# Large loads of a cached-attention decode kernel carried half by SyncE's queue and half by ScalarE's

## The chip, the cores and the metric

The kernel runs on one core of a Trainium2 chip. The metric is the device time of one execution in microseconds (us), taken as the median over runs. The engines are named as in the profile: PE is TensorE, DVE is VectorE, ACT is ScalarE, POOL is GpSimd, SP is SyncE. A transfer (DMA) is issued by an engine's instruction stream, here by SP's or ACT's, and is carried by 16 DMA engines that all transfers of the core share. Each issuing engine has one queue on each DMA engine. "Entries" below are what such a queue holds: one packet for each contiguous row of a transfer that falls to that DMA engine, and one more that counts the transfer's semaphore up.

## The reference, cut to what matters

One decode step (one query token for each of two sequences) of grouped attention over a long cache, times a gated small network:

```python
# x: (2, 1, 512); k_cache, v_cache: (2, 8, 32768, 128) bf16, 134 MB each
xn = layernorm(x)
q  = xn @ wq                                   # 32 heads of 128; 4 heads share one of the 8 cache heads
scores = einsum("bhqd,bhkd->bhqk", q, k) * 128 ** -0.5
o  = einsum("bhqk,bhkd->bhqd", softmax(scores), v)
s  = o.reshape(2, 1, 4096) @ wo                # wo: 4096 x 512
# B, with one token: the shifted quarters of its first stage are all zero, so x1 = xn
b  = xn + gelu(layernorm(xn) @ w3) @ w4        # w3: 512 x 1792, w4: 1792 x 512
out = x + s * silu(b)
```

Nearly all bytes are K and V, each read once: 280.5 MB in all with the weights.

## The kernel before, in words

There are 16 groups, one for each pair of sequence and cache head. A group's K is 32768 x 128 bf16, which is 8 MB: 128 partitions of 64 KB each, cut into two parts of 32 KB (`NPART = 2`, a part is a `SLOT`). Its V has the same shape. `kbuf` has three slots, so the next group's K can be loaded as soon as the first part of the present one is used up; `vbuf` has two, so the next V waits until the present V is used up.

For each group DVE transposes K in 16 pieces (line 493), PE multiplies them with the query (line 562, scores in `sc`), DVE finds the maximum (lines 476 to 503), ACT takes the exponential (line 417), DVE transposes the result (line 511), PE multiplies with V (line 584, sum in `o`), and ACT copies `o` out to `ob` (line 420). PE's part of a group is one loop body that is run 16 times. After the last group PE multiplies the collected outputs with `wo` (lines 608 and 615), DVE makes the last two products (lines 520 and 521), and SP and ACT each store one row.

All large loads are issued by SP, in the order of the code, each behind the event that frees its buffer:

- at the start `wq`, `w3`, `w4` and K of group 0, with no wait (lines 252 to 255). `wq` lies in the third slot of `kbuf`; `w3` and `w4` lie in `vbuf`.
- V of group 0 behind `e_h2`, the last matmul that reads `w4` (line 387).
- K of group m behind `s_half` reaching m: PE gives it when it has used the first part of K of group m - 1 (line 398).
- V of group m behind `s_pv` reaching m: PE gives it when it has used V of group m - 1 (line 387).
- K and V of the last group as two parts each (lines 404 and 392), and then `wo` in seven parts (line 411), which lies where K was.

ACT issues small transfers only: `x` (line 258), four pieces of `x` spread over partitions into `x4_bf` (line 270, "x4" below; two rows of 256 bytes each), four pieces of the gate `g` into `g4` (line 379; two rows of 512 bytes each), and half of the output. The engines' instruction streams run in order. DVE's stream has, between the prologue and its loop over the groups, a copy of `x4_bf` that waits for the four x4 transfers (line 380), and behind it two memsets (lines 381 and 382), of which PE's loop waits for the second:

```python
e_x4 = ve.op(lambda v: v.tensor_copy(out=x4[:, :], in_=x4_bf[:, :]), (d_x4, 16 * NQ))
ve.op(lambda v: v.memset(qrb[:, :], 0.0), e_qr)
e_s0 = ve.op(lambda v: v.memset(pro[:, :], 0.0))
```

DVE's loop then begins a group by waiting for K's semaphore `t_k[i]`. A transfer adds 16 to its semaphore, one for each DMA engine, and `take(..., 16)` waits for that and subtracts it.

Of the kernel before, what the change touches and what calls it, by code (L numbers as in the profile page):

```python
# [94 lines left out]
def kernel(  # L95
# [14 lines left out]
    nc = tc.nc  # L110

    B, Sq, D = A_x.shape
    _, Hkv, Sk, Dh = A_k_cache.shape
    HD = A_wq.shape[1]
# [94 lines left out]

    groups = [(b, k) for b in range(B) for k in range(Hkv)]  # L210
    NG = len(groups)
    wo_parts = [(0, 4, 0, NQ), (4, 5, 0, NQ), (5, 6, 0, NQ), (6, 7, 0, NQ), (7, 8, 0, 2), (7, 8, 2, 3), (7, 8, 3, NQ)]
    KC = 2
    PAD = 24

    def sem(name):
        return tc.alloc_semaphore(name)
# [1 line left out]
    def row_view(cache, b, k):  # L219
        return cache[b, k, :, :].rearrange("(p t) d -> p (t d)", p=128)  # L220
# [26 lines left out]
    def order(m):  # L247
        return (1, 0) if m % 2 == 0 else (0, 1)

    with tc.tile_critical(sync_engine=mybir.EngineType.Pool, no_gpsimd_drain=True):  # L250

        sp.op(lambda e: e.dma_start(out=kbuf_wq[:, 0:DK * HD], in_=A_wq.rearrange("(p k) f -> p (k f)", k=DK)), inc=(d_wq, 16))
        sp.op(lambda e: e.dma_start(out=vbuf[:, 0:W4O], in_=B_w3.rearrange("(p k) f -> p (k f)", k=DK)), inc=(d_w3, 16))
        sp.op(lambda e: e.dma_start(out=vbuf[:, W4O:W4O + FK * D], in_=B_w4.rearrange("(p f) d -> p (f d)", f=FK)), inc=(d_w4, 16))
        sp.op(lambda e: e.dma_start(out=kbuf[:, 0:NPART * SLOT], in_=row_view(A_k_cache, *groups[0])), inc=(t_k[0], 16))
        nc.sync.sem_inc(t_k[1], 16)

        ac.op(lambda e: e.dma_start(out=x_bf[:, :], in_=A_x[:, 0, :]), inc=(d_x, 16))
        e_x4z = po.op(lambda e: e.memset(x4_bf[:, :], 0.0))
        e_xs0 = po.op(lambda e: e.memset(xs_bf[:, :], 0.0))  # L260
        e_id0 = po.op(lambda e: e.memset(ident[:, :], 0.0))
# [70 lines left out]
        for i in range(NPART):  # L332
            for k in range(DK):
                for n in range(NQ):
                    last = k == DK - 1 and n == NQ - 1
                    e = pe.op(lambda t, i=i, k=k, n=n: t.matmul(  # L336
                        sc[i][32 * n:32 * n + B, :], lhsT=xT[:, k, :],
                        rhs=wq3[:, k, :].rearrange("p (h n y) -> p h n y", n=NQ, y=32)[:, i * HH:(i + 1) * HH, n, :],
                        start=(k == 0), stop=(k == DK - 1), tile_position=(0, 32 * n)),
                        e_xT, e_s00, (d_wq, 16), inc=last)  # L340
            e = ve.op(lambda v, i=i: v.transpose(out=qT[:, i * 512:(i + 1) * 512], in_=sc[i][:, :]), e)
        e_q = ve.op(lambda v: v.tensor_mul(
            out=q_sb[:, :, :, :].rearrange("p n e (b h) -> p (n e) b h", b=B),
# [10 lines left out]
        for k in range(DK):  # L354
            for n in range(NQ):
                last = k == DK - 1 and n == NQ - 1
                e = pe.op(lambda t, k=k, n=n: t.matmul(
                    pro[32 * n:32 * n + B, 0:FQ], lhsT=xT[:, DK + k, :],
                    rhs=w3v[:, k, n * FQ:(n + 1) * FQ].rearrange("p (y f) -> p f y", y=32),
                    start=(k == 0), stop=(k == DK - 1), tile_position=(0, 32 * n)), (d_w3, 16), inc=last)  # L360
        e = ve.op(lambda v: v.transpose(out=h4[:, :], in_=pro[:, 0:FQ]), e)
        e_hf = ve.op(lambda v: v.tensor_copy(
            out=hf[:, :].rearrange("p (f b) -> p f b", b=B), in_=h4[:, :].rearrange("p (f c) -> p f c", c=32)[:, :, 0:B]), e)
# [7 lines left out]
        for f in range(FK):  # L371
            e_h2 = pe.op(lambda t, f=f: t.matmul(  # L372
                h2[0:B, :], lhsT=h_bf[:, f * B:(f + 1) * B], rhs=w4v[:, f, :],
                start=(f == 0), stop=(f == FK - 1)), e, (d_w4, 16), inc=f == FK - 1)
        e_tf = ve.op(lambda v: v.tensor_add(out=t_f[:, :], in0=xn[:, :], in1=h2[0:B, :]), e_h2)
        e = ac.op(lambda v: v.activation(out=sig[:, :], in_=t_f[:, :], func=ACT.Sigmoid), e_tf)
        e_g = ve.op(lambda v: v.tensor_mul(out=g[:, :], in0=t_f[:, :], in1=sig[:, :]), e)
        for n in range(NQ):
# [3 lines left out]
        e_s0 = ve.op(lambda v: v.memset(pro[:, :], 0.0))  # L382


        def load_v(m, *events):
            if m < NG - 1:
                sp.op(lambda e: e.dma_start(out=vbuf[:, :], in_=row_view(A_v_cache, *groups[m])), *events, inc=(t_v[0], 16))
                nc.sync.sem_inc(t_v[1], 16)
                return
            for h in range(NPART):  # L390
                c = slice(h * SLOT, (h + 1) * SLOT)
                sp.op(lambda e, c=c: e.dma_start(out=vbuf[:, c], in_=row_view(A_v_cache, *groups[m])[:, c]), *events, inc=(t_v[h], 16))  # L392

        load_v(0, e_h2)
        for m in range(1, NG):
            base = m % 2
            if m < NG - 1:
                sp.op(lambda e, m=m, base=base: e.dma_start(
                    out=kbuf[:, base * SLOT:(base + NPART) * SLOT], in_=row_view(A_k_cache, *groups[m])),
                    (s_half, m), e_q, inc=(t_k[0], 16))  # L400
                nc.sync.sem_inc(t_k[1], 16)
            else:
                for i, h in enumerate(order(m)):
                    sp.op(lambda e, m=m, h=h, base=base: e.dma_start(
                        out=kbuf[:, (base + h) * SLOT:(base + h + 1) * SLOT],
                        in_=row_view(A_k_cache, *groups[m])[:, h * SLOT:(h + 1) * SLOT]),
                        (s_half, m), inc=(t_k[i], 16))
            load_v(m, (s_pv, m))
        for i, (a, c, r0, r1) in enumerate(wo_parts):
            cols = slice(r0 * D, r1 * D)  # L410
            sp.op(lambda e, a=a, c=c, cols=cols: e.dma_start(out=wo3[:, a:c, cols], in_=wos[:, a:c, cols]), (s_pv, NG - 1), inc=(d_wo[i], 16))  # L411


        for m in range(NG):
            for h in range(NPART):
                i = order(m).index(h)
                ac.op(lambda v, i=i: v.activation(  # L417
                    out=ep[i][:, :], in_=sc[i][:, :], func=ACT.Exp, scale=inv_sqrt_dh, bias=shift[:, :], accum_out=rs[:, i:i + 1]),
                    (s_shift, m + 1), e_tf if m == 0 else None, inc=(t_e, 1))
            ac.op(lambda v: v.copy(out=ob[:, :], in_=o[:, :]), (s_pv, m + 1), inc=(t_ob, 1))  # L420

        z_cols = z[:, :, :, (NR - 1) * rep:].rearrange("p n e c -> p (n e) c")
        z_cols = z_cols[:, :, 0:128].rearrange("p w (j c) -> p w j c", j=4)[:, :, :, 0:rep]
# [58 lines left out]
        with nc.Fori(0, NG // 2, engines=[DVE], hint_back_edge=True):  # L482
            for par in range(2):
                take(nc.vector, t_z)
                for i, h in enumerate(order(par)):
                    take(nc.vector, t_k[i], 16)
                    u = par + h
                    kt = kbuf[:, u * SLOT:(u + 1) * SLOT].bitcast(I32)
                    for r in range(NR):
                        n = i * NR + r  # L490
                        if n >= T_BUFS:
                            take(nc.vector, t_used)
                        nc.vector.transpose(  # L493
                            out=Ts[n % T_BUFS][:, :].rearrange("p (b t k) -> p t b k", b=NB, t=RT),
                            in_=kt[:, r * W:(r + 1) * W].rearrange("p (t b k) -> p t b k", b=NB, t=RT)).then_inc(t_T, 1)
                        if i == 1 and r == 3:
                            peak(0)
                            head_on()
                head_out()
                take(nc.vector, t_used, T_BUFS)  # L500
                peak(1)
                take(nc.vector, t_top)
                nc.vector.tensor_reduce(  # L503
                    out=shift[:, :], in_=S[:, NPART * rep:], axis=AX.X, op=ALU.min).then_inc(s_shift, 1)
                for h in range(NPART):
                    take(nc.vector, t_e)
                    if h == NPART - 1:
                        nc.vector.tensor_mul(
                            out=sm[:, :, :], in0=sel_h[:, :].unsqueeze(1).broadcast_to([128, NPART, rep]),
                            in1=rs[:, :].unsqueeze(2).broadcast_to([128, NPART, rep]))  # L510
                    nc.vector.transpose(  # L511
                        out=pt[h][:, :, :].rearrange("p r (t h) -> p t r h", h=rep),
                        in_=ep[order(par).index(h)][:, :].rearrange("p (t r h) -> p t r h", r=NR, h=rep)).then_inc(t_pt, 1)
# [36 lines left out]
        with nc.body("pe_groups", valid_engines=[PE]):  # L550
# [24 lines left out]
                S[:, NPART * rep:], lhsT=same_h[:, :], rhs=mxr[:, :, :].rearrange("p i r -> p (i r)"),  # L575
                start=True, stop=True).then_inc(t_top, 1)
            for h in range(NPART):
                take(nc.tensor, t_v[h], 16)
                take(nc.tensor, t_pt)
                vt = vbuf[:, h * SLOT:(h + 1) * SLOT].rearrange("p (t d) -> p t d", d=Dh)  # L580
                for u in range(KPT // VT):
# [16 lines left out]
        with nc.body("pe_output", valid_engines=[PE]):  # L598
# [3 lines left out]
            for i, (a, c, r0, r1) in enumerate(wo_parts):  # L602
                for k in range(a, c):
                    pe.wait(e_oX[(B - 1) * Hkv + k], (d_wo[i], 16))
                    for r in range(r0, r1):
# [7 lines left out]
                        for n in range(NQ):  # L613
# [2 lines left out]
                                pro[32 * n:32 * n + B, 0:QW], lhsT=oX[:, k, r, :], rhs=wo3[:, k, col:col + QW],  # L616
                                start=(gr == KC * NQ), stop=(gr == Hkv * NQ - 1), tile_position=(0, 32 * n)),
                                inc=(gr == Hkv * NQ - 1 and n == NQ - 1))
                if i == 0:
                    take(nc.tensor, t_on)  # L620
                    head_xp()
                    for n in range(NQ):
# [41 lines left out]
```

## Time and profile before

| What | Value |
|---|---|
| median of 3 runs | 658.0 us (657.98 to 658.12) |
| the profiled execution | 657.31 us |
| its span, first to last instruction | 655.5 us |
| HBM read | 280.50 MB, 428 GB/s over the span |
| PE busy / DVE busy / ACT busy | 62% / 58% / 6% of the span |
| packets of SP's queue (q1) | 6728, 280.50 MB, 99.0% of 16 engines' span |
| packets of ACT's queue (q10) | 44, 0.01 MB |
| mean granted clock of PE | 0.81 |

The page gives busy time by engine, the span in 40 slices with the share of the DMA engines and their rate, the DMA queues, the chain of work that ended last, the costliest groups of instructions, and the DMA issues. The timeline lists single instructions with their start and duration and, in brackets, the idle time before them and what ended it. Below the page, the trace has a record of every DMA packet (queue, start, duration, size) and of every increment by which a transfer closes on a DMA engine; "the packet records" and "the landing records" are these.

### The profile page before, as it was taken

The page shows a single profiled execution, that of the slowest core. Times are in us where ns is not written, and L with a number is a line of the kernel's source. Part 1 is how long each engine was busy: PE and PEld are TensorE (multiplying, and loading weights), DVE is VectorE, ACT ScalarE, POOL GpSimd, SP SyncE. Part 2 cuts the span into 40 slices and gives each one's busy share as a digit, 9 for nine tenths or more (in the row PEclk, how much of TensorE's full clock was granted, in tenths as well). Part 3 has the DMA queues.
Part 4 walks back from the last instruction along what each step waited for, and adds up shares of the span by engine and source line. Part 5 has one row for each costly group of instructions (what it writes and reads, how often), then busy time and mean ns, then how long its engine had stood idle before and what let it go on. Part 6 is the DMA issues. An engine that isn't in the chain of part 4 may idle for free. (4 is left out here: it accounts for less than half of the span.)

```text
span 655.5 us, 6482 instructions
## 1 busy us (share of the span) xinstructions
PE 409.6 (62%) x2444; PEld 164.1 (25%) x2444; DVE 380.2 (58%) x534; ACT 39.5 (6%) x89; POOL 10.1 (2%) x43
## 2 busy tenths in 40 slices
PE   2528386564938656494765749566383856648765
PEld 0113132231313212131321313232131322213323
DVE  5348194673819457291855729285482937638770
ACT  1100101000010000001000000100001010000100
POOL 1000000000000000000000000000000000000000
PEclk9859677696987769697686969878696887979798
DMA  8999999999999999999999999999999999999996
GB/s 365 435 449 444 445 420 420 444 444 444 396 448 444 444 428 412 448 440 444 416 428 444 440 448 400 444 444 440 440 404 448 440 444 420 424 444 414 448 418 262
DMA packets 6779, 280.58 MB, mean 428 GB/s; under 512 B 746, under 2 KB 1012, under 8 KB 2036
## 3 DMA queue, kind: packets, MB, share of 16 engines
q1 hardware_dynamic: 6728, 280.50, 99.0%
q8 instruction: 2, 0.03, 0.0%
q14 instruction: 5, 0.04, 0.0%
q10 hardware_dynamic: 44, 0.01, 0.0%
HBM read 280.50 MB, written 0.00 MB: 428 GB/s over the span
## 5 line engine op out<-in xcount | busy, mean ns | idle before, releaser
L493 DVE STREAM_TRANSPOSE T<-kbuf 128x1024 int32<-128x1024 int32 x256 | 295.7, 1214 | 186.7 <-DVEq L473 186.4
L562 PE MATMUL sc<-T,z 128*128 128x512 bf16 x1024 | 280.2, 422 | 164.9 <-PEq L473 161.8
L562 PEld LDWEIGHTS sc<-T,z 128*128 128x128 bf16 x1024 | 98.8, 104 | 330.1 <-issue 251.7
L584 PE MATMUL o<-vbuf,pt 128*16 128x512 bf16 x1024 | 90.8, 533 | 35.0 <-PEq L473 35.0
L584 PEld LDWEIGHTS o<-vbuf,pt 128*16 128x16 bf16 x1024 | 34.3, 117 | 85.8 <-issue 78.4
L417 ACT ACTIVATE ep<-sc,shift 128x512 bf16<-128x512 f32 x32 | 21.7, 682 | 479.8 <-DVE shift L503 479.8
L511 DVE STREAM_TRANSPOSE pt<-ep 128x512 bf16<-128x512 bf16 x32 | 22.6, 708 | 15.3 <-DVEq L473 15.3
L476 DVE TENSOR_REDUCE mx<-sc 128x1 f32<-128x512 f32 x32 | 21.5, 672 | 15.7 <-DVEq L473 15.7
L574 PE MATMUL S<-mxr,same_h 128*128 128x64 f32 x32 | 6.5, 284 | 22.0 <-PEq L473 22.0
L532 PEld LDWEIGHTS oT<-sel_o,ob 128*128 128x128 f32 x136 | 17.7, 191 | 3.2 <-issue 0.5
L532 PE MATMUL oT<-sel_o,ob 128*128 128x4 f32 x136 | 16.2, 243 | 0.5 <-PEq L473 0.5
L420 ACT COPY ob<-o 128x512 f32<-128x512 f32 x16 | 9.4, 585 | 97.0 <-PE o L584 97.0
L574 PEld LDWEIGHTS S<-mxr,same_h 128*128 128x128 f32 x32 | 4.8, 188 | 29.8 <-issue 29.8
L438 POOL COPY oX<-oXs 128x4 bf16<-128x4 bf16 x15 | 2.8, 188 | 520.8 <-DVE oXs L470 520.8
L478 DVE TENSOR_SCALAR mxr<-row_of,mx 128x32 f32<-128x32 f32 x32 | 7.7, 241 | 4.8 <-DVEq L473 0.3
L503 DVE TENSOR_REDUCE shift<-S 128x1 f32<-128x64 f32 x16 | 3.6, 225 | 11.2 <-DVEq L473 11.2
L591 PEld LDWEIGHTS S<-sm,ones_f 128*128 128x128 f32 x32 | 4.8, 188 | 6.9 <-issue 6.9
L372 PE MATMUL sc<-vbuf,h_bf 128*2 128x512 bf16 x14 | 4.8, 521 | 2.4 <-DVE h_bf L369 2.4
L417 ACT ACTIVATION_READ_ACCUMULATOR ep<-sc,shift 128x1 f32 x32 | 6.3, 196 | 0.0
L427 POOL TENSOR_TENSOR z<-qr,quad 128x64 bf16<-128x64 bf16 x16 | 4.7, 292 | 102.2 <-DVE shift L503 86.4
L591 PE MATMUL S<-sm,ones_f 128*128 128x8 f32 x32 | 6.2, 266 | 0.0
L336 PE MATMUL sc<-kbuf,xT 128*2 128x512 bf16 x32 | 3.6, 627 | 4.1 <-DMA kbuf<-in_A_wq_dram 4.1
(88 smaller groups left out, 63.6 us busy)
## 6 DMA issues: line engine op xcount, KB each, us to landing
kbuf<-in_A_k_cache_dram SPq DMA_DIRECT2D x2, 4096.0 KB, 21.7
vbuf<-in_A_v_cache_dram SPq DMA_DIRECT2D x2, 4096.0 KB, 20.2
kbuf<-in_A_wq_dram SPq DMA_DIRECT2D x1, 4096.0 KB, 12.3
vbuf<-in_B_w_dram SPq DMA_DIRECT2D x2, 1792.0 KB, 18.0
kbuf<-in_A_wo_dram SPq DMA_DIRECT2D x1, 2048.0 KB, 29.3
kbuf<-in_A_wo_dram SPq DMA_DIRECT2D x3, 512.0 KB, 30.8
kbuf<-in_A_wo_dram SPq DMA_DIRECT2D x1, 256.0 KB, 31.7
kbuf<-in_A_wo_dram SPq DMA_DIRECT2D x2, 128.0 KB, 15.6
```

What stands on the lines that cost most here:

```text
L372: e_h2 = pe.op(lambda t, f=f: t.matmul(h2[0:B, :], lhsT=h_bf[:, f * B:(f + 1) * B], rhs=w4v[:, f, :], start=(f == 0), stop=(f == FK - 1)), ...
L417: ac.op(lambda v, i=i: v.activation(out=ep[i][:, :], in_=sc[i][:, :], func=ACT.Exp, scale=inv_sqrt_dh, bias=shift[:, :], accum_out=rs[:, i ...
L420: ac.op(lambda v: v.copy(out=ob[:, :], in_=o[:, :]), (s_pv, m + 1), inc=(t_ob, 1))
L476: nc.vector.tensor_reduce(out=mx[:, i:i + 1], in_=sc[i][:, :], axis=AX.X, op=ALU.max).then_inc(t_d, 1)
L478: ins = nc.vector.tensor_scalar_mul(out=mxr[:, i, :], in0=row_of[:, :], scalar1=mx[:, i:i + 1])
L493: nc.vector.transpose(out=Ts[n % T_BUFS][:, :].rearrange("p (b t k) -> p t b k", b=NB, t=RT), in_=kt[:, r * W:(r + 1) * W].rearrange("p (t ...
L511: nc.vector.transpose(out=pt[h][:, :, :].rearrange("p r (t h) -> p t r h", h=rep), in_=ep[order(par).index(h)][:, :].rearrange("p (t r h) ...
L532: ins = nc.tensor.matmul(oT[:, :], lhsT=ob[:, t * Dh:(t + 1) * Dh], rhs=sel_o[:, t, :], start=(t == 0), stop=(t == VT - 1))
L562: ins = nc.tensor.matmul(sc[i][:, :], lhsT=z[:, nb, w, zc:zc + 128], rhs=Tb[:, nb, :, w], start=(r == 0 and nb == 0 and w == 0), stop=(r = ...
L574: nc.tensor.matmul(S[:, NPART * rep:], lhsT=same_h[:, :], rhs=mxr[:, :, :].rearrange("p i r -> p (i r)"), start=True, stop=True).then_inc( ...
L584: ins = nc.tensor.matmul(o[32 * j:32 * j + VT * rep, :], lhsT=pt[h][:, r, a * VT * rep:(a + 1) * VT * rep], rhs=vt[:, u * VT:(u + 1) * VT, ...
L591: nc.tensor.matmul(S[:, 0:NPART * rep], lhsT=ones_f[:, :], rhs=sm[:, :, :].rearrange("p i h -> p (i h)"), start=True, stop=True).then_inc( ...
```

## The change

A helper `load` issues the left half of every row on SP's queue or the right half on ACT's. Every large load is issued by both, behind the same event, and its semaphore now takes 32. At the start SP's stream is `wq`, `w3`, `w4`, K of group 0 (halves), and ACT's stream is `x`, then the other halves of those four, and then the four x4 transfers. In the loop ACT issues its half of the next K ahead of the exponentials of a group, and its half of the next V ahead of the copy to `ob`. The last K and V are four transfers each. `wo` has ten parts in place of seven: part i is issued by SP where i is even and by ACT where it is odd. The matmul that finishes the last head in the output stage stands behind the second part of `wo`, which with the first is what the first part was. `PAD` (waits that fill PE's stream ahead of the end) goes from 24 to 22.

```diff
-    wo_parts = [(0, 4, 0, NQ), (4, 5, 0, NQ), (5, 6, 0, NQ), (6, 7, 0, NQ), (7, 8, 0, 2), (7, 8, 2, 3), (7, 8, 3, NQ)]
+    wo_parts = [(0, 2, 0, NQ), (2, 4, 0, NQ), (4, 5, 0, NQ), (5, 6, 0, NQ), (6, 7, 0, 2), (6, 7, 2, NQ)] + [(7, 8, r, r + 1) for r in range(NQ)]
-    PAD = 24
+    PAD = 22
...
-        sp.op(lambda e: e.dma_start(out=kbuf_wq[:, 0:DK * HD], in_=A_wq.rearrange("(p k) f -> p (k f)", k=DK)), inc=(d_wq, 16))
...
-        nc.sync.sem_inc(t_k[1], 16)
+        def load(q, dst, src, s_, *events):
+            def half(ap):
+                n = ap.shape[-1] // 2
+                return ap[:, 0:n] if q is sp else ap[:, n:]
+            q.op(lambda e: e.dma_start(out=half(dst), in_=half(src)), *events, inc=(s_, 16))
 
         ac.op(lambda e: e.dma_start(out=x_bf[:, :], in_=A_x[:, 0, :]), inc=(d_x, 16))
+        for q in (sp, ac):
+            load(q, kbuf_wq[:, 0:DK * HD], A_wq.rearrange("(p k) f -> p (k f)", k=DK), d_wq)
+            load(q, vbuf[:, 0:W4O], B_w3.rearrange("(p k) f -> p (k f)", k=DK), d_w3)
+            load(q, vbuf[:, W4O:W4O + FK * D], B_w4.rearrange("(p f) d -> p (f d)", f=FK), d_w4)
+            load(q, kbuf[:, 0:NPART * SLOT], row_view(A_k_cache, *groups[0]), t_k[0])
+        nc.sync.sem_inc(t_k[1], 32)
...
         for n in range(NQ):
             ac.op(lambda e, n=n: e.dma_start(out=x4_bf[32 * n:32 * n + B, :], in_=A_x[:, 0, n * QW:(n + 1) * QW]), e_x4z, inc=(d_x4, 16))
...
+        def load_k(q, m):
+            base = m % 2
+            if m < NG - 1:
+                load(q, kbuf[:, base * SLOT:(base + NPART) * SLOT], row_view(A_k_cache, *groups[m]), t_k[0], (s_half, m), e_q)
+                if q is sp:
+                    nc.sync.sem_inc(t_k[1], 32)
+                return
+            for i, h in enumerate(order(m)):
+                load(q, kbuf[:, (base + h) * SLOT:(base + h + 1) * SLOT],
+                     row_view(A_k_cache, *groups[m])[:, h * SLOT:(h + 1) * SLOT], t_k[i], (s_half, m))
+        def load_v(q, m, *events):
...
+        def load_wo(q):
+            for i, (a, c, r0, r1) in enumerate(wo_parts):
+                cols = slice(r0 * D, r1 * D)
+                if q is (sp, ac)[i % 2]:
+                    q.op(lambda e, a=a, c=c, cols=cols: e.dma_start(out=wo3[:, a:c, cols], in_=wos[:, a:c, cols]), (s_pv, NG - 1), inc=(d_wo[i], 16))
+        load_v(sp, 0, e_h2)
+        for m in range(1, NG):
+            load_k(sp, m)
+            load_v(sp, m, (s_pv, m))
+        load_wo(sp)
+        load_v(ac, 0, e_h2)
         e = ac.op(lambda v: v.activation(out=sig[:, :], in_=t_f[:, :], func=ACT.Sigmoid), e_tf)
...
         for m in range(NG):
+            if m < NG - 1:
+                load_k(ac, m + 1)
             for h in range(NPART):
                 i = order(m).index(h)
                 ac.op(lambda v, i=i: v.activation(
...
+            if m < NG - 1:
+                load_v(ac, m + 1, (s_pv, m + 1))
             ac.op(lambda v: v.copy(out=ob[:, :], in_=o[:, :]), (s_pv, m + 1), inc=(t_ob, 1))
+            if m == NG - 2:
+                load_wo(ac)
...
-                    take(nc.vector, t_k[i], 16)
+                    take(nc.vector, t_k[i], 32)
...
-                if i == 0:
+                if i == 1:
                     take(nc.tensor, t_on)
                     head_xp()
```

More of the change, by code (lines that the diff above doesn't have):

```diff
@@ L250 @@
     with tc.tile_critical(sync_engine=mybir.EngineType.Pool, no_gpsimd_drain=True):
[L252 to L255, printed above, removed]
-        nc.sync.sem_inc(t_k[1], 16)
-        ac.op(lambda e: e.dma_start(out=x_bf[:, :], in_=A_x[:, 0, :]), inc=(d_x, 16))
+        def load(q, dst, src, s_, *events):
[3 more added lines that the diff above has]
+            q.op(lambda e: e.dma_start(out=half(dst), in_=half(src)), *events, inc=(s_, 16))
+        ac.op(lambda e: e.dma_start(out=x_bf[:, :], in_=A_x[:, 0, :]), inc=(d_x, 16))
+        for q in (sp, ac):
[4 more added lines that the diff above has]
+        nc.sync.sem_inc(t_k[1], 32)
         e_x4z = po.op(lambda e: e.memset(x4_bf[:, :], 0.0))
@@ L339 @@
                         start=(k == 0), stop=(k == DK - 1), tile_position=(0, 32 * n)),
-                        e_xT, e_s00, (d_wq, 16), inc=last)
+                        e_xT, e_s00, (d_wq, 32), inc=last)
             e = ve.op(lambda v, i=i: v.transpose(out=qT[:, i * 512:(i + 1) * 512], in_=sc[i][:, :]), e)
@@ L359 @@
                     rhs=w3v[:, k, n * FQ:(n + 1) * FQ].rearrange("p (y f) -> p f y", y=32),
-                    start=(k == 0), stop=(k == DK - 1), tile_position=(0, 32 * n)), (d_w3, 16), inc=last)
+                    start=(k == 0), stop=(k == DK - 1), tile_position=(0, 32 * n)), (d_w3, 32), inc=last)
         e = ve.op(lambda v: v.transpose(out=h4[:, :], in_=pro[:, 0:FQ]), e)
@@ L373 @@
                 h2[0:B, :], lhsT=h_bf[:, f * B:(f + 1) * B], rhs=w4v[:, f, :],
-                start=(f == 0), stop=(f == FK - 1)), e, (d_w4, 16), inc=f == FK - 1)
+                start=(f == 0), stop=(f == FK - 1)), e, (d_w4, 32), inc=f == FK - 1)
         e_tf = ve.op(lambda v: v.tensor_add(out=t_f[:, :], in0=xn[:, :], in1=h2[0:B, :]), e_h2)
+        def load_k(q, m):
[10 more added lines that the diff above has]
+            if m < NG - 1:
+                load(q, vbuf[:, :], row_view(A_v_cache, *groups[m]), t_v[0], *events)
+                if q is sp:
+                    nc.sync.sem_inc(t_v[1], 32)
+                return
+            for h in range(NPART):
+                c = slice(h * SLOT, (h + 1) * SLOT)
+                load(q, vbuf[:, c], row_view(A_v_cache, *groups[m])[:, c], t_v[h], *events)
+        def load_wo(q):
[9 more added lines that the diff above has]
+        load_v(ac, 0, e_h2)
         e = ac.op(lambda v: v.activation(out=sig[:, :], in_=t_f[:, :], func=ACT.Sigmoid), e_tf)
@@ L382 @@
         e_s0 = ve.op(lambda v: v.memset(pro[:, :], 0.0))
-        def load_v(m, *events):
+        for m in range(NG):
             if m < NG - 1:
[L387 to L414, printed above, removed]
+                load_k(ac, m + 1)
             for h in range(NPART):
@@ L577 @@
             for h in range(NPART):
-                take(nc.tensor, t_v[h], 16)
+                take(nc.tensor, t_v[h], 32)
                 take(nc.tensor, t_pt)
```

## The prediction

> **What bounds the kernel now.** I read the page's slices and queues first, then the chain that ended last, then the timeline of the first 60 us, and last the packet and landing records.
>
> The page's rows of the DMA engines' busy share and of their rate by slice, and the rows of the two issuing queues:
>
> ```profile
> DMA  8999999999999999999999999999999999999996
> GB/s 365 435 449 444 445 420 420 444 444 444 396 448 444 444 428 412 448 440 444 416 428 444 440 448 400 444 444 440 440 404 448 440 444 420 424 444 414 448 418 262
> ...
> q1 hardware_dynamic: 6728, 280.50, 99.0%
> ...
> q10 hardware_dynamic: 44, 0.01, 0.0%
> ```
>
> The reader is to see that the DMA engines never rest between the first slice and the last, and that one queue, q1 (SP's), fills them. The dips in the rate are no rest: the landing records close an 8 MB load on a given engine every 19.32 us through the whole loop. The first packet of q1 starts at 1.93, the last piece of `wo` lands at 649.6 to 651.2, by engine. So this is a transfer-bound kernel: its time is start, entries on one DMA engine, idle time of the DMA engines (now none), and a tail.
>
> The end of the chain of waits (start, duration, what):
>
> ```profile
> 618.33 0.42 SPq L411
> 618.75 0.05 issue
> 618.80 13.43 SPq L411
> 632.22 0.04 issue
> 632.26 6.31 SPq L411
> 638.58 0.04 issue
> 638.62 12.61 DMA kbuf<-in_A_wo_dram
> 651.23 0.04 issue
> 651.27 0.26 PE pro L615 x4
> ```
>
> The last thing waited for is the last piece of `wo`. SP's issues of `wo` stood 13.43 and 6.31 us because its queue was full, which cost nothing: data was queued all the while.
>
> The timeline of the start (start, duration, engine, line, what):
>
> ```profile
> 0.89 0.39 SPq L252 DMA_DIRECT2D kbuf<-in_A_wq_dram  x1
> 0.90 0.55 ACTq L258 DMA_DIRECT2D x_bf<-in_A_x_dram  x1
> 1.50 1.24 ACTq L270 DMA_DIRECT2D x_bf<-in_A_x_dram  x4
> ...
> 29.20 0.33 SPq L387 DMA_DIRECT2D vbuf<-in_A_v_cache_dram  x1
> ...
> 31.19 0.21 DVE L380 CAST x<-x_bf 128x128 f32<-128x128 bf16 x1
> ...
> 32.04 0.48 DVE L382 MEMSET pro<- 128x512 f32 x1
> ...
> 42.12 5.78 DVE L493 STREAM_TRANSPOSE T<-kbuf 128x1024 int32<-128x1024 int32 x5 [9.60 <-DVEq L473]
> ...
> 53.39 0.33 SPq L398 DMA_DIRECT2D kbuf<-in_A_k_cache_dram  x1
> ```
>
> DVE does the x4 copy (L380) at 31.19 and then waits 9.60 us for K of group 0; 11.27 us after its first transpose the load of K of group 1 goes out. V of group 0 lands at 59.5 to 60.1, on the slowest engine at 60.8, so that issue is about 6 us ahead of need.
>
> **The change part by part.** *Bandwidth.* The same bytes pass the same 16 engines, which are full, so two queues bring no bytes forward. What changes is the number of entries. Per DMA engine a load of 8 packets of 64 KB and one count becomes 16 of 32 KB and two counts: 9 more. Three weights 27, thirty full loads 270, the last K and V (four transfers become eight) 36, `wo` (87 become 106) 19: 352 more. Price: the last K and V already go as halves with 32 KB packets, and close every 9.68 us. Two of them take 19.36 against 19.32, so 0.04 us for 9 entries, 4.4 ns each: 352 x 4.4 ns = 1.6 us. Upper bound: a 32 KB packet takes 1213 ns and a 64 KB one 2418, so 8 ns for a cut, 352 x 8 = 2.8 us. Lower bound, because no row has two queues full at once: if the second queue fills the gaps at packet borders, all 420 present entries lose their 4.4 ns, a gain of 1.9 us. I take 1.6, the row of the same packet size.
>
> The Trainium skill, page "DMA: Bandwidth & Descriptors", section "Rules for kernel authors", says that spreading transfers over several issuing engines does not help bandwidth, since all run on the same 16 engines. The full DMA row above bears it out; by that rule alone the sum would be the entries' price.
>
> *The start: x4 goes behind K.* ACT's x4 issues (L270, 1.50 now) move behind four halves on ACT's queue: `wq`, `w3`, `w4`, K of group 0. Each queue is served in its order on every engine, so x4 comes after ACT's half of K, which ends when K ends (40.1 to 40.7 now, slowest 41.5). SP's queue by then holds its half of V of group 0 (issued 29.20). How two queues share an engine is in the packet records: the g4 entries, issued from 31.35, come on one engine at 35.63, 38.07, 40.49, 43.08, 45.50, 47.93, 50.35 and 52.79, 2.43 us apart, which is one 64 KB packet of SP's queue between any two, counts included. So the eight entries of x4 (four data, four counts) wait for eight V packets of 32 KB: 8 x 1.21 = 9.7 us, from about 40.3 to 50.0. Lower bound zero, if they leave before V; upper 11.
>
> Nothing covers that: DVE's copy of x4 stands in its stream ahead of the transposes. Landing 0.3 and waking 0.1: the copy at 50.4 in place of 31.19. Copy and two memsets take 32.52 - 31.19 = 1.33: the first transpose at 51.8 in place of 42.12. K of group 1 then goes out at 51.8 + 11.3 = 63.1. First byte after an issue: 1.93 - 0.89 = 1.04, so 64.1. V of group 0 ends at 60.2 (0.1 to 0.2 later for the entries so far), on the slowest engine at 61.0. The DMA engines idle 3.9 us, the slowest 3.1. V of group 1: before, 73.51, 31.4 us after the first transpose; after, 83.2, first byte 84.2; K of group 1 ends at 64.1 + 19.4 = 83.5: idle 0.7. From there the margin holds: in group 1 the issues come 11.9 and 32.9 us after the first transpose (81.07, 92.94, 113.99 now), so 96.2 and 117.2 against data that ends at 103.6 and 123. Idle 4.6 us on most engines, 3.8 on the slowest, which sets the end but whose lag partly arises later: I take 4.2, bounds 0 and 6.
>
> *Moved past ACT's other work.* Four issues of 0.4 to 0.5 us, about 2.0 together, stand ahead of ACT's first table load (1.28 us, from 2.77 to 4.05 now), so it ends near 6.05 and the first square root comes 1.2 us after its present 4.86. The chain behind it ends at 10.73, and PE waits for `wq` until 13.27: 2.5 us of cover. The sigmoid's table load (1.28, at 23.77 now) comes behind the issue of V at 29.2, so the gate is some 0.9 us later, which the x4 wait hides, and without that the wait for K until 42.1. In the loop the K half is issued while ACT is idle (it waits 31 us for `shift`), and the V half puts the copy to `ob` 0.4 us later, which PE needs some 20 us on. g4 lies behind V's half, and in the idle stretch leaves quickly; it is needed at the end alone. All at nothing. SP's stream does the same number of large issues, and two fewer of `wo`.
>
> *The tail.* `wo` now leaves from two queues, 53 entries each, and the last two quarters of the last part land together: eight matmuls of L615 behind the last landing in place of four (0.26): +0.25.
>
> *Sum.* 657.3 + 1.6 + 4.2 + 0.25 = 663.35. The profiled execution is 0.7 below the median of the runs: 664.0.
>
> **The rivals.** *Small transfers are not late* (0.14 of the chance). If an engine takes x4 with K's half in one turn, DVE starts at 42.1, no idle time arises, and what is left is 1.6 + 0.25: 659.9. Against it stand the 2.43 us between g4's entries. The Trainium skill, same page, section "Queues, rings and completion order", lets an engine drain a packet of some 9 to 17 descriptors from one queue before it turns to the next, by which x4 could go at once. The trace does not agree: one row of 64 KB stands between any two entries of g4.
>
> *Faster: the second queue fills the gaps and x4 isn't late* (0.09). Place: the 420 packet borders on each engine, 1.9 us; 658.0 - 1.9 + 0.25 = 656.4. It decides from where x4 lands before about 46 us, because then K of group 1 still goes out before V ends. For it: nothing shows two full queues. Against it: a rate that already stands within 0.5% of that inside a packet.
>
> *A lower rate* (0.08). Two streams of rows on each engine cost 1% where no row bounds it: 664.0 + 6.5 = 670.5.
>
> *ACT is held at a full queue* (0.07). SP's seventh open `wo` issue stood until 638.6. If ACT's five behave so, its last exponentials (636.69) come up to 3.4 us later, and the last head's matmuls (L615 at 648.8) end at 652.2, one us behind `wo`: 665.2. Against: counted from the code, each queue holds about 75 entries there, and SP's held about 80 before it stood.
>
> **How the numbers follow.** Forecast 0.62 (its own range 661.5 to 666), the rivals 0.14, 0.09, 0.08, 0.07. A measurement tells 0.2% (1.3 us) from no change: 656.7 to 659.3 is "same". The small-transfers case lies at 659.9 and falls on both sides of that bound, half of it "same". So faster 0.09, same 0.07, slower 0.84. The range runs from 659.2 (that case's near end) to 667.5, leaving out the faster case and the lower rate.
>
> **What would show it.** DVE's copy of x4 at about 50 and the first transpose at about 52; a wait of DVE for x4 of some 18 us; K of group 1 issued near 63; a hole in the DMA rate near 61 to 64 and a small one near 84, and none later; q1 and q10 with about half the packets each; the period of a group 38.7 us as before, longer by 0.08 at most; SP no longer standing in L411; eight matmuls behind the last landing. Wrong it is if DVE starts at 42 (then x4 overtook), if the period of a group changes by over 0.2 us (then two queues change the rate), or if K's landing drifts behind V's in the loop (then the queues fall out of step).

## The result and the profile after

The changed kernel takes 666.57 us (median of 4 runs, 665.87 to 668.25) against 657.99 us for the kernel before on the same chip: a ratio of 1.0139, 95% interval 1.0127 to 1.0151, so 8.6 us slower. The prediction was 664.0, with 661.5 to 666 for its own mechanism and 659.2 to 667.5 in all; the measured time is inside the second and 0.6 above the first. The profiled execution took 665.87 us, its span 664.1.

The page's busy share and rate of the DMA engines by slice, and the two queues, of the kernel after:

```profile
DMA  8997999999999999999999999999999999999996
GB/s 361 443 428 285 441 403 432 430 436 430 434 432 436 434 428 435 430 438 430 434 434 432 434 428 438 430 434 434 434 432 434 432 430 436 432 436 424 427 432 261
...
q1 hardware_dynamic: 6184, 140.25, 49.2%
q10 hardware_dynamic: 6220, 140.26, 49.2%
```

The bytes are now shared evenly by the two queues, in nearly twice the packets. The row that was nines from its second slice on has a 7 in its fourth, at 285 GB/s. The sixth slice, at 403 GB/s, holds a second and smaller hole that the digits don't show; the slices behind it are as full as before.

The start in the timeline of the kernel after:

```profile
0.89 0.40 SPq L257 DMA_DIRECT2D kbuf<-in_A_wq_dram  x1
...
1.50 0.37 ACTq L257 DMA_DIRECT2D kbuf<-in_A_wq_dram  x1
...
3.53 1.29 ACTq L279 DMA_DIRECT2D x_bf<-in_A_x_dram  x4
...
26.57 5.47 PE L381 MATMUL sc<-vbuf,h_bf 128*2 128x512 bf16 x14 [3.79 <-DMA vbuf<-in_B_w_dram]
32.06 0.33 SPq L257 DMA_DIRECT2D vbuf<-in_A_v_cache_dram  x1
...
50.99 0.23 DVE L424 CAST x<-x_bf 128x128 f32<-128x128 bf16 x1 [15.88 <-DMA x_bf<-in_A_x_dram]
...
52.41 5.78 DVE L515 STREAM_TRANSPOSE T<-kbuf 128x1024 int32<-128x1024 int32 x5
...
63.67 0.33 SPq L257 DMA_DIRECT2D kbuf<-in_A_k_cache_dram  x1
...
83.79 0.33 SPq L257 DMA_DIRECT2D vbuf<-in_A_v_cache_dram  x1
```

The x4 transfers are issued at 3.53 behind ACT's four halves; DVE waits 15.88 us for them ahead of its copy of x4 (L424), which runs at 50.99 in place of 31.19. The first transpose comes at 52.41, SP's half of K of group 1 goes out at 63.67 and ACT's at 63.61. Busy time by stretch (columns: stretch, length, then busy us and count for PE, PEld, DVE, ACT and POOL, the granted clock, the share of the DMA engines, GB/s; a packet counts in the stretch in which it starts), kernel after:

```profile
60.00:62.00 2.00, 2.00 (x10) 0.77 (x8) 2.00 (x2) 0.00 (x0) 0.00 (x0) 1.00 0.00 0
62.00:64.00 2.00, 1.89 (x9) 0.83 (x9) 2.00 (x3) 0.00 (x0) 0.00 (x0) 1.00 0.00 0
64.00:66.00 2.00, 2.00 (x15) 1.34 (x14) 2.00 (x3) 1.28 (x1) 0.00 (x0) 1.00 0.99 262
66.00:84.00 18.00, 12.92 (x96) 5.01 (x95) 9.50 (x19) 1.45 (x4) 0.29 (x1) 0.91 1.01 434
84.00:86.00 2.00, 0.07 (x1) 0.00 (x0) 0.00 (x0) 0.59 (x1) 0.00 (x0) 0.96 0.74 229
86.00:88.00 2.00, 0.00 (x0) 0.00 (x0) 0.80 (x1) 0.00 (x0) 0.00 (x0) 0.50 0.88 360
```

No packet with data starts from 60 to 64, and there is a second, shallower hole from 84 to 88. Set against the kernel before, the last count of V of group 0 comes 0.3 us earlier, of K of group 1 6.1 later, of V of group 1 7.5, and of the last piece of `wo` 8.5 (landing records of both: 61.0, 87.1, 107.8, 659.7 against 61.3, 80.9, 100.2, 651.2). Most is lost in the two holes; behind V of group 1 it grows by another 1.0. The end of the chain of the kernel after (start, duration, what):

```profile
625.18 0.42 SPq L411
...
625.65 33.90 DMA kbuf<-in_A_wo_dram
...
659.60 0.47 PE pro L637 x6
```

It still ends with the last piece of `wo`, no issue of `wo` stands any more, and the matmuls behind it take 0.47 in place of 0.26.

### The profile page after: what moved, and what is told of

It is laid out like the page before. It is cut to its first block, busy times and chain, and to the rows that moved or that the text cites. A ratio compares the mean times of both kernels' runs of the same rounds, so it can differ in the third digit from the quotient of the medians.

```text
span 664.1 us, 6490 instructions
## 1 busy us (share of the span) xinstructions
PE 399.5 (60%) x2412; PEld 163.2 (25%) x2444; DVE 379.7 (57%) x534; ACT 39.5 (6%) x89; POOL 10.2 (2%) x43
## 5 line engine op out<-in xcount | busy, mean ns | idle before, releaser
L584 PE MATMUL sc<-T,z 128*128 128x512 bf16 x992 | 270.9, 417 | 182.1 <-PEq L495 177.9
L606 PE MATMUL o<-vbuf,pt 128*16 128x512 bf16 x1024 | 89.2, 526 | 35.1 <-PEq L495 35.1
L424 DVE CAST x<-x_bf 128x128 f32<-128x128 bf16 x1 | 0.2, 227 | 15.9 <-DMA x_bf<-in_A_x_dram 15.9
L467 DVE TENSOR_REDUCE den<-S 128x4 f32<-128x8 f32 x17 | 2.7, 159 | 6.2 <-DVEq L495 6.2
## 6 DMA issues: line engine op xcount, KB each, us to landing
kbuf<-in_A_k_cache_dram SPq DMA_DIRECT2D x15, 4096.0 KB, 26.1
vbuf<-in_A_v_cache_dram ACTq DMA_DIRECT2D x15, 4096.0 KB, 26.5
vbuf<-in_A_v_cache_dram SPq DMA_DIRECT2D x2, 2048.0 KB, 20.5
```

The costliest lines, as they stand in the source:

```text
L584: ins = nc.tensor.matmul(sc[i][:, :], lhsT=z[:, nb, w, zc:zc + 128], rhs=Tb[:, nb, :, w], start=(r == 0 and nb == 0 and w == 0), stop=(r = ...
L606: ins = nc.tensor.matmul(o[32 * j:32 * j + VT * rep, :], lhsT=pt[h][:, r, a * VT * rep:(a + 1) * VT * rep], rhs=vt[:, u * VT:(u + 1) * VT, ...
```

## The experiments

Times are set against runs of the kernel before on the same chip, whose median was 657.52 to 657.63 us. Two theories and two rivals went in. X: the late x4 holds DVE, and the DMA engines run dry. Entries: every cut of a packet has a price. Q: two full queues on an engine cost by themselves. S: ACT's issues in the loop hold its other work.

**x4 issued first (a1).** In the changed kernel:

```diff
         ac.op(lambda e: e.dma_start(out=x_bf[:, :], in_=A_x[:, 0, :]), inc=(d_x, 16))
+        e_x4z = po.op(lambda e: e.memset(x4_bf[:, :], 0.0))
+        for n in range(NQ):
+            ac.op(... x4_bf[32 * n:32 * n + B, :] ..., e_x4z, inc=(d_x4, 16))
         for q in (sp, ac):
             load(...)
```

> The changed kernel with one thing moved: ScalarE issues the four x4 transfers right behind x, ahead of its halves of wq, w3, w4 and K. Theory X (x4 behind K holds VectorE, and the DMA engines run dry): the first transpose of K at 42 to 43 in place of 52.4, no hole in the DMA rate, and 658.0 + 1.6 (entries) + 0.25 (tail) = 659.9 us, 659.3 to 660.5. Rival Q (two full queues on an engine cost by themselves, wherever x4 stands): 664 to 667. Rival S (ScalarE's issues in the loop hold its exponentials or copies): 664 to 667.

659.50 us, 2.0 over the kernel before; ratio 1.0028 (1.0017 to 1.0040). The timeline of this kernel:

```profile
38.94 0.21 DVE L424 CAST x<-x_bf 128x128 f32<-128x128 bf16 x1
...
43.62 5.78 DVE L515 STREAM_TRANSPOSE T<-kbuf 128x1024 int32<-128x1024 int32 x5 [3.34 <-DVEq L495]
...
55.40 0.36 ACTq L257 DMA_DIRECT2D kbuf<-in_A_k_cache_dram  x1
```

The copy of x4 no longer waits, DVE waits for K as before, K of group 1 goes out at 55.40, and of the 8.6 us 6.6 are gone by one moved statement. That is theory X's number; rivals Q and S are ruled out as the main cost, since queues, halves and ACT's issues in the loop are untouched. The moved statement did a little more than take the wait away: K of group 0 also closes earlier here, at 43.5 in place of 45.9 (landing records). The next run separates the two.

**The copy of x4 behind the loop (a2).** x4 stays late, the wait is taken off DVE's path:

```diff
-        e_x4 = ve.op(lambda v: v.tensor_copy(out=x4[:, :], in_=x4_bf[:, :]), (d_x4, 16 * NQ))
...
+        e_x4 = ve.op(lambda v: v.tensor_copy(out=x4[:, :], in_=x4_bf[:, :]), (d_x4, 16 * NQ))
         head_on(last=True)
```

> The changed kernel with VectorE's copy of x4 moved behind its loop over the groups, where it first is needed; the x4 transfers stay where the change put them and land as late. Theory X: the wait is what costs, not the transfers: first transpose at 42 to 43, 659.9 us, 659.3 to 660.5. Rival E (the eight x4 entries on the queue of two DMA engines hold K or V themselves): over 663. Rival Q and rival S: 664 to 667.

661.04 us, 3.5 more than the kernel before; ratio 1.0064 (1.0049 to 1.0080). 5.1 of the 8.6 us are gone although x4 lands as late as in the changed kernel (last count at 51.2), so the wait is the main cause and not the transfers; but it is over 1 us more than theory X gave. The timeline shows why:

```profile
46.68 5.78 DVE L514 STREAM_TRANSPOSE T<-kbuf 128x1024 int32<-128x1024 int32 x5 [11.36 <-DVEq L494]
...
57.94 0.36 ACTq L257 DMA_DIRECT2D kbuf<-in_A_k_cache_dram  x1
```

The first transpose waits until 46.68 for K itself (42.12 before). The landing records close SP's half of K of group 0 at 35.9 to 36.2 and ACT's at 45.6 to 46.5. The packet records show where that comes from: SP's queue starts first, and on every engine five of its packets pass before the first of ACT's (80 on the 16 engines); from there the queues take turns by packet, whatever its size, so that SP is already at K's 32 KB packets while ACT still brings `w4` in 7 KB ones. The late x4 covered this second delay in the changed kernel. So 5.1 of the 6.6 us that a1 won back are the wait for x4; the rest goes with K of group 0 closing late.

**Halves on one queue (b1).** The kernel before, each large load but `wo` cut in two:

```diff
+        def halves(dst, src, s_, *events):
+            n = dst.shape[-1] // 2
+            sp.op(lambda e: e.dma_start(out=dst[:, 0:n], in_=src[:, 0:n]), *events, inc=(s_, 16))
+            sp.op(lambda e: e.dma_start(out=dst[:, n:], in_=src[:, n:]), inc=(s_, 16))
```

> The kernel before, with every large load but wo as two halves of each row, both on SyncE's queue: the changed kernel's packets without its second queue and without a late x4. Entries theory: 333 more entries on each DMA engine at 4.4 ns are 1.5 us, so 659.5 us (upper bound 8 ns each: 660.7). If entries cost nothing: 658.0.

658.98 us, 1.44 more; ratio 1.0023 (1.0014 to 1.0033). With 333 more entries that is 4.3 ns each (2.8 to 6.5 by the interval), against 4.4 in the prediction. The price of the cut is there without a second queue. The period of a group, from the landing records of groups 3 to 13, says the same and settles rival Q for the loop: 38.64 us in the kernel before, 38.73 here with halves on one queue, and 38.73 with halves on two (the changed kernel, a1 and c1 below).

**x4 late in the kernel before (b2).**

```diff
-            ac.op(... x4_bf ..., e_x4z, inc=(d_x4, 16))
...
+            ac.op(... x4_bf ..., e_x4z, e_h2, inc=(d_x4, 16))
         e = ac.op(... sig ..., e_tf)
```

> The kernel before, one queue and whole rows, with the four x4 transfers issued only behind the last matmul that reads w4 (29.2 us). Theory X: their eight entries then alternate with packets of 64 KB, 8 x 2.43 us, and land near 53; first transpose near 54.4, K of group 1 out near 65.7, a hole of about 6 us in the DMA rate and a smaller one near 86: 658.0 + 8 = 666 us, 664.5 to 667.5, without any split of the loads. Rivals Q and S: 658.0, as the loads are untouched.

663.55 us, 6.0 more, with a wide spread (660.06 to 667.20; the profiled run is the 667.20); ratio 1.0076 (1.0053 to 1.0099). In its timeline:

```profile
50.57 0.23 DVE L380 CAST x<-x_bf 128x128 f32<-128x128 bf16 x1 [17.03 <-DMA x_bf<-in_A_x_dram]
51.98 5.78 DVE L493 STREAM_TRANSPOSE T<-kbuf 128x1024 int32<-128x1024 int32 x5
...
63.83 0.33 SPq L398 DMA_DIRECT2D kbuf<-in_A_k_cache_dram  x1
```

One queue, whole rows, and the loss is of the same kind. The median lies 1 us below the range given. Single runs differ by 7 us; in the profiled one, the longest, one DMA engine stays about 3 us behind the middle one through the loop (1.4 in the kernel before, landing records), which is part of it. Why an engine falls behind in some runs stays open.

**DVE late by itself (d1, d2, d4).** To size the loss without touching any transfer, memsets of a scratch tile stand ahead of DVE's loop in the kernel before, 36, 27 or 19 of them:

```diff
         e_s0 = ve.op(lambda v: v.memset(pro[:, :], 0.0))
+        dly = sb("dly", [128, 512], F32)
+        for _ in range(36):
+            e_s0 = ve.op(lambda v: v.memset(dly[:, :], 0.0), e_s0)
```

> The kernel before, one queue, whole rows, x4 early, with 36 memsets of a scratch tile on VectorE ahead of its loop, so that its first transpose comes near 52 as in the changed kernel (42.1 before). Theory X: the whole cost of the late x4 is the late VectorE, so +6 to +7 us over the kernel before, as much as the changed kernel lost against the one with x4 first; K of group 1 goes out near 63.5 and the DMA engines run dry there. If my prediction's sizes of the hole were right: +4.2. Rival E (the x4 entries themselves hold the data of two DMA engines): clearly less than +4.

> The same with 27 memsets, so that the first transpose comes near 47 to 48. Theory X with the margin that I read from the trace (K of group 1 goes out some 6 us ahead of need): it goes out at 58.5 to 59, its first byte at 59.5 to 60 while V of group 0 ends at 60.1 to 60.8, so no hole or hardly one: 0 to +0.8 us. If lateness costs from the first microsecond: +2.5 or more.

> The run with 27 memsets put VectorE's first transpose at 50.25, later than was meant, and K of group 1 out at 62.20: it lost 5.9 us. With 19 memsets (0.62 us each) the first transpose comes near 45.3 and K of group 1 goes out near 57. The kernel with 27 showed what a restart takes: 1.0 us from issue to first byte and 0.7 us that the first packet is longer. V of group 0 ends at 59.6 to 60.7, so up to an issue at 58 nothing should be lost. If that is the margin: 0 to +0.4 us over the kernel before. If lateness costs from the first microsecond (about 0.9 us for each, as between the runs with 27 and 36): +3.

The memsets started 0.66 us apart, more than I had reckoned, so the transposes began later than meant in d1 and d2. "K1 out" is the issue of K of group 1, "V1 out" that of V of group 1, from the timelines of the profiled runs; the times are medians of all runs:

| kernel | first transpose | K1 out | V1 out | time over the kernel before | ratio |
|---|---|---|---|---|---|
| before | 42.12 | 53.39 | 73.51 | 0 | |
| 19 memsets (d4) | 45.08 | 56.87 | 77.77 | 0.5 | 1.0011 (1.0002 to 1.0020) |
| 27 memsets (d2) | 50.25 | 62.20 | 83.23 | 5.9 | 1.0082 (1.0066 to 1.0098) |
| 36 memsets (d1) | 55.84 | 66.80 | 86.92 | 10.3 | 1.0150 (1.0131 to 1.0168) |

Lateness is nearly free up to an issue near 57 and then costs about 1 us for each: (10.3 - 5.9) / (66.80 - 62.20) = 0.96. At 63.67, where the changed kernel issues, the line gives 0.5 + 6.8 x 0.96 = 7.0; the changed kernel lost 6.6 against the one with x4 first. So a late DVE alone is enough to account for it. The line is good to 1 or 2 us only: the profiled runs, to which the issue times belong, took 659.52, 664.70 and 667.58 us, up to 1.5 off their medians. With that margin it fits the others: a2 issues at 57.94, 1.5 us on the line and 1.4 for entries, 2.9, and measured 3.5.

The kernel with 27 memsets also shows the holes cleanly, in the same columns as above:

```profile
60.00:62.00 2.00, 2.00 (x11) 0.83 (x10) 2.00 (x3) 0.00 (x0) 0.00 (x0) 1.00 0.00 0
62.00:64.00 2.00, 2.00 (x15) 1.42 (x14) 2.00 (x3) 0.00 (x0) 0.00 (x0) 1.00 1.45 492
...
82.00:84.00 2.00, 1.50 (x22) 0.59 (x14) 0.00 (x0) 0.58 (x1) 0.00 (x0) 0.91 0.09 33
84.00:86.00 2.00, 0.00 (x0) 0.00 (x0) 0.42 (x1) 0.00 (x0) 0.00 (x0) 0.94 1.48 492
```

The packet records put V of group 0's end at 59.5 to 60.1 on most engines and the restart at 63.2 to 63.7, with a first packet of 2.7 to 3.3 us in place of 2.42; K of group 1 ends at 83.1 to 83.7 on most, and the second restart comes at 84.2 to 84.7, with a first packet of 2.6 to 3.5 us. As a mean over the 16 engines the first hole is 3.6 us and the long packets behind it cost 0.6, the second hole is 1.0 and its long packets 0.7: 6.0 us, where the kernel's median lost 5.9. This profiled run lost 7.1; in it the last engine is 2.4 us behind the middle one in the loop, against 1.4 before, which is the remaining 1 us.

**The loop alone on two queues (c1).** The changed kernel with the start of the kernel before (`wq`, `w3`, `w4`, K of group 0 whole on SP):

> The changed kernel with the start of the kernel before: wq, w3, w4 and K of group 0 whole and on SyncE's queue alone, x and x4 alone on ScalarE's; V of group 0 and all later loads in halves on both queues, wo in ten parts. Theory X with entries: no late x4, no hole, and the entries of the loop (some 316 at 4.4 ns, 1.4 us) plus a tail of up to 0.25: 1.4 to 1.7 us over the kernel before. A rival by which the first kernel with x4 first still paid for its uneven start (its K of group 0 closed on ScalarE's side 8 us after SyncE's) expects this one below that kernel's +2.0. A rival by which two queues in the loop cost by themselves expects +2 or more.

659.54 us, 2.0 more by the medians; the ratio, 1.0042 (1.0029 to 1.0055), says 1.9 to 3.6. K of group 0 is whole on SP's queue here and still on its way when ACT's half of V goes out at 29.31; the two take turns, and K lands at 44.2 to 45.7, where it landed at 40.4 to 42.0. So K of group 1 goes out at 57.08, by the line 0.7 us, and entries are 1.4. It does not come out below the kernel with x4 first: another start, about the same price. The time alone would also fit the rival by which two queues in the loop cost by themselves; the period of a group, 38.73 us as with halves on one queue (b1), speaks against it.

**Split by partitions (c2).** On top of the loop-only kernel:

```diff
             def half(ap):
-                n = ap.shape[-1] // 2
-                return ap[:, 0:n] if q is sp else ap[:, n:]
+                return ap[0:64, :] if q is sp else ap[64:128, :]
```

> The same start as the loop-only kernel, but each load is split by partitions: SyncE's queue carries partitions 0 to 63 and ScalarE's 64 to 127, whole rows, so two queues with 64 KB packets (10 entries in place of 9 for a load on each DMA engine). If only entries cost: 34 of them, 0.15 us, and the tail, so +0.2 to +0.4 us over the kernel before. If the second queue fills the gaps at packet borders: -1 to -1.9 us. If two queues cost by themselves: +1.5 or more.

1270.64 us (1238.12 to 1292.46), nearly twice the time, which no theory had. A stretch of this kernel (the run of 1292.46), in the same columns:

```profile
200.00:400.00 200.00, 61.51 (x321) 25.08 (x327) 58.47 (x72) 4.07 (x10) 0.97 (x4) 0.62 1.01 215
```

and the same stretch of the kernel before:

```profile
200.00:400.00 200.00, 133.07 (x730) 52.69 (x728) 120.26 (x157) 10.15 (x25) 2.40 (x10) 0.77 1.00 431
```

The engines are just as busy and move half the bytes, here and in the later stretches (213 to 215 GB/s, against 431 to 435): a 64 KB packet takes 4.9 us (median) in place of 2.42. The Trainium skill, page "SBUF — State Buffer", section "Door 1: The DMA port swizzle", says that partitions 0 to 63 reach only 8 of the 16 ports and gives about 218 GB/s as the limit for them. The 213 to 215 measured here agree, although the other half was on the other queue at the same time. That the engines serve one half and then the other in step would be an explanation, but the packet records speak against it: packets of both queues are under way at once in four of five samples, and a packet takes 4.8 to 5.0 us whether 2 or 16 of the packets under way are its own queue's. Why stays open. Whether a second queue fills the gaps at packet borders could not be told from this run.

**`wo` alone on two queues (c3).** The kernel before with the change's `wo_parts` and `load_wo`:

> The kernel before with the part of the change that concerns wo alone: ten parts in turn on the two queues, ScalarE's five behind the copy to ob of group 14. The term of the tail: 19 entries (0.1 us) and eight matmuls behind the last landing in place of four (0.25): +0.2 to +0.4 us. A rival by which ScalarE is held at a full queue: +1 to +2, with its last exponentials late.

659.17 us (657.91 to 660.54), 1.65 more; ratio 1.0026 (1.0017 to 1.0035), more than the tail term. ACT was not held: its five issues take 2.39 us at 614.47. With K and V on SP alone ACT's queue is empty there, so its `wo` parts do not queue behind the last V but share the engines with it: the first lands at 638, before the last V, and the last V lands at 644.3 where it landed at 641.2. The chain then runs through PE:

```profile
648.91 1.84 PE oT L537 x8
...
651.71 0.85 PE pro L620 x32
```

So this run does not measure the tail of the changed kernel, where both queues hold V; it shows what an empty second queue does.

**`wo` on SP alone, x4 first (d3).**

> The kernel with x4 first on both queues (+2.0 us over the kernel before when it was run), with wo in seven parts on SyncE's queue alone as before. If the tail term was right, 0.25 to 0.5 us less than that kernel: +1.4 to +1.7, which is the price of the entries. If the tail costs more than I said: +1.0 or less. If the rest above the entries lies in the two queues: +2.0.

659.42 us, 1.8 more; ratio 1.0027 (1.0016 to 1.0038), against 1.0028 with `wo` on both queues. The two do not differ beyond their intervals, so the tail's size stays open.

**x4 between ACT's halves of `w4` and K (c4).** The same four issues, one load earlier than in the change:

> The changed kernel with the four x4 transfers between ScalarE's halves of w4 and of K of group 0, so behind three halves but not the fourth. Theory X: what matters is that SyncE's 32 KB packets of V do not stand between the eight entries; here packets of K do, so x4 lands near 35 to 40, ahead of K, and there is no wait: +1.5 to +2.5 us over the kernel before. If any place behind the big halves is too late: +5 or more.

660.13 us, 2.6 more by the medians; the ratio, 1.0053 (1.0034 to 1.0071), says 2.2 to 4.7. x4 lands at 28.5 to 31.7 and DVE does not wait for it. What remains is the uneven start as in a2: K of group 1 goes out at 57.86, 1.4 on the line, and 1.4 for entries. What made the change slow was, for the most part, x4's place behind K.

No kernel here beats the one before: its DMA engines had no idle time to win back, and every form of the split added entries.

## Why the prediction was right, and what was off

The mechanism came true, and 664.0 against 666.57 is near; but the rise was forecast as 6.0 us and was 8.6, and one of the times in between came out right by luck.

*Bandwidth, and the entries.* Right: the loop's rate did not rise, the period of a group went from 38.64 to 38.73 us, and the term of 1.6 us stands at 1.44 in the run with one queue (for 333 of the 352 entries). The lower bound (gaps filled by the second queue) did not come about in any kernel with halves on both.

*x4 behind K.* Right in place and cause, and in the times that follow: copy at 50.4 and measured at 50.99, first transpose 51.8 and 52.41, K of group 1 out at 63.1 and 63.67, V of group 1 out at 83.2 and 83.79. But that x4 was through at 50.0 (50.1 measured) is luck, two errors that cancel. The step had ACT's half of K end near 40.3, with K as in the kernel before, and then eight packets of V, 9.7 us. In the packet records ACT's half of K ends at 45.1 to 45.6, since the two queues' halves drifted apart; x4's entries on its two DMA engines then come at 46.4, 47.6, 48.8 and 50.0, one V packet of 1.21 us before each, and all the others follow at once, up to 50.1, because SP's half of V ended on these two engines at 50.0. So the start was 5 us later and the turns were four, not eight. And x4 was not the whole delay: without the wait for it, DVE would have begun at 46.68 (a2) and not at 42.12.

*The idle time.* Here the size failed: 4.2 us in the sum, 6.6 measured against the kernel with x4 first. The step took from the issue to the first byte (1.04, right) and then let the engines run at once at full pace. In the packet records of the kernel after, as means over the 16 engines, the first hole is 4.8 us (4.1 to 5.2), not 3.9, since V of group 0 ended at about 59.9, not 60.2, and K went out 0.6 us later than said. The first 32 KB packet behind it takes 1.7 to 2.2 us, not 1.21, which costs 0.8 and was in no term. The second hole is 0.6, near the 0.7 in the sum, and the long packets behind it cost 0.5. Together 6.7. With 1.5 for entries and 0.2 for the tail that is 8.4 of the 8.6 us. The margin was misread with it: I set the issue at 53.39 against V's end near 60 and called it 6 us. With 1.04 to the first byte it is about 5, and the next load is tighter: V of group 1 goes out at 73.51, its first byte is due at 74.55, and K of group 1 ends at 78.8, so about 4. The profiled run with 19 memsets, which issues K of group 1 3.5 us later than the kernel before and V of group 1 4.3, was at that edge: no hole ahead of K, and 0.3 us and long packets ahead of V.

*Moved past ACT's other work.* The first square root came at 6.15 (6.05 given) and was covered. Not covered was something I had not listed, the two queues' halves drifting apart: ACT's half of `w4` landed at 26.1 to 26.5, and PE waited 3.79 us for it, so V of group 0 went out 2.9 us later than before. In the changed kernel that lay under the x4 wait.

*The tail.* Eight matmuls in place of four would be 0.25; the chain shows 0.47 for six records against 0.26 for four, and the run with `wo` on SP alone (1.0027 against 1.0028) could not tell the whole of it from zero.

*The rivals.* Small transfers did wait, one packet for each entry, counts included, as long as SP's queue held packets on their engines, so the case of x4 in one turn did not come about; a lower rate did not either, by the period of a group. ACT was not held at a full queue: its exponentials of the last group (645.07) follow `shift` at once.

## What to carry to other kernels

A queue serves its transfers in order, so a small transfer that something waits for is best issued ahead of the large ones on the same queue; four transfers of half a kilobyte, issued 2 us later, cost 5 us here by themselves, and 6.6 with what else moved. Where the DMA engines are full, a second queue adds no rate, and each cut of a row adds an entry with a price. What cost most here were moments in which nothing was queued, so for every load compare its issue with the end of the data ahead of it, and take the tightest of the following loads, not the first. One late instruction of an engine with 58% busy time was enough to empty the queues, and what was lost at the start of this full pipeline did not come back. Two halves of a load on two queues need not end together either, and whoever waits for the load waits for the later one.

## What was not expected of the hardware

- A queue that starts while another is streaming gets its first turn late: 4.2 us after the issue for ACT's half of `wq` (1.50 to 5.65; 80 packets of 16 KB of SP's started first, five for each engine), 5.0 for x4 in the kernel before (1.50 to 6.50), 3.8 for ACT's half of V in c1 (29.31 to 33.14), against 1.0 onto idle engines.
- Turns go by packet and not by byte, so the lead grows where packet sizes differ: `wq` closed 3.5 us apart, K of group 0 9.7 us apart. From 20.5 to 25.5, 50 packets of 32 KB start on SP's queue and 48 of 7 KB on ACT's.
- After idle time the first packet takes longer than the later ones, by 0.4 to 1.0 us for 32 KB (1.21 in the stream) behind the first hole of the kernel after, and by 0.2 to 0.9 for 64 KB (2.42 in the stream) on 15 of 16 engines behind that of d2, on top of 1.0 us from the issue.
- Halves by partition on two queues ran at 213 to 215 GB/s, halves by column at 434, with the DMA engines fully busy in both.
